# A third order for the repeated part of a linear-attention and ELU feed-forward kernel on one core

## The chip, the cores and the metric

One NeuronCore of one Trainium2 chip runs the program. The metric is device time in microseconds (us) of one execution; the span is the part of it between the first and the last instruction of the profile. Engines: TensorE (PE, its weight loads PEld), VectorE (DVE), ScalarE (ACT), GpSimd (POOL), SyncE (SP), which here only issues DMAs.

## The reference

Gated linear attention over 768 steps for 4 batches and 8 heads of width 48, then a feed-forward layer with an ELU on the 3072 tokens of width 384. All in float32.

```python
for t in range(S):                                   # q, k, v, alpha: (4, 8, 768, 48)
    state = alpha[:, :, t, :, None] * state + einsum('bhd,bhe->bhde', k[:, :, t], v[:, :, t])
    y[:, :, t] = einsum('bhd,bhde->bhe', q[:, :, t], state)
x = y.transpose(0, 2, 1, 3).reshape(3072, 384)
h = x @ w_in                                         # 384 x 2048
g = where(h > 0, h, exp(minimum(h, 0)) - 1)
out = g @ w_out                                      # 2048 x 384
```

## The kernel before

The sequence is cut into 24 windows of 128 steps (6 for each batch), handled in chunks of 64; the tokens into 12 blocks of 256, two windows each, and the hidden width into 8 pieces j of 256. Each step of the work is a small function, a token. A program text is a list of tokens with their index; START holds the tokens of the first part one by one, STEADY (L79) is a pattern that `steady()` (L761) repeats for g = 4 to 13 and that is cut off at both ends. Under `manual_schedule` each engine runs its instructions in the order of the list; between engines only data, buffers and semaphores order the work. So the list is ten queues of order at once, one for each engine, and the place of a token against tokens of other engines has no force by itself.

In STEADY the number behind a token counts from g: for A, RA, RB, RC, GH, GL and O it is 8 g + k, the piece j of a block (A.0 to A.4 are pieces 0 to 4 of block g, A.-3 to A.-1 pieces 5 to 7 of block g - 1; O.-5 is piece 3 of block g - 1); for CA, CB and LC it is 4 g + k; for Z it is the block; for the others the window 2 g + k.

The tokens, with their engine and line:

- Loads on SP, all on one queue in list order: L (L170, k, q and alpha of a window), LV (L183, v, two DMAs), LC (L593, a part of the weights, read again for a check), XD (L536, four small copies that fold y into the layout of x), Z's two stores (L709).
- Window work: SC (DVE, L195, a scan of alpha into P), LN and EX (ACT, L208, L213), KA and KB (POOL here, L221, L226), KC (DVE, L231), SQ (POOL here, L240), T.i.g (DVE, L288, four transposes of 32 x 32 blocks by its helper; four T a window), PC (ACT, L236, a sum for a check), ZV (POOL, L264).
- S (PE, L328) and U (PE, L374), 32 small matmuls each, write the two halves of the same two PSUM banks of a window. MK (DVE, L344, in two parts of two instructions) masks what S gave. UA, UB, UC (DVE, L416 to L428, two instructions each) form the state for the second chunk and for the next window from what U gave. UA of each sixth window is on ACT.
- Y (PE, L483, 32 matmuls), XH (ACT, L501) and XL (DVE, L521) make the two float32r halves of the feed-forward input xt of a block.
- Feed-forward: A (PE, L640, 18 matmuls of 128 x 256 into one bank h), RA and RB (ACT, L655, L661), RC (DVE, L666), GH (ACT, L672), GL (DVE in all blocks from 4 on, L682), O (PE, L692, 12 matmuls of 128 x 384 into the two banks of a block), Z (ACT and SP, L709).
- CA and CB (ACT, L599, L604) check the weights that LC loaded. V and VP come once, in block 11.

Buffers: one pool of 8 PSUM banks serves h, y, the pairs of U and S and the pairs of O; r, gh and gl have three buffers each (gh and gl are free again when their O has run), ck has one, P, R, kn, y3 and xt two, qka tiles three and v tiles four in rotation.

```python
h = psa.tile([128, 2, BLK], F32, name="h", tag="pa")                       # A
gh = d["gh"] = gpool.tile([128, 2, BLK], F32R, name="gh", tag="gh", bufs=3)  # GH
gl = d["gl"] = gpool.tile([128, 2, BLK], F32R, name="gl", tag="gl", bufs=3)  # GL
```

Of the kernel before, what the change touches and what calls it, by code (L numbers as in the profile page):

```python
# [14 lines left out]
B, H, S, D = 4, 8, 768, 48  # L15
# [61 lines left out]


STEADY = """  # L79
A.-3 Y.1 XH.1 Y.0 XH.0 A.-2 XL.1 RA.-3 O.-5 RA.-2 XL.0 LV.4 U.2 CA.-12 V.0 RB.-3 S.2 UA.2 MK.2.0 U.3 UB.2 S.3  # L80
MK.2.1 UC.2 XD.1 ZV.4 O.-4 XD.0 RC.-3 CB.-12 SC.4 RB.-2 A.-1 PC.3 GH.-3 RC.-2 A.0 LN.4 GL.-3 UA.3 EX.4 RA.-1
GH.-2 LC.-11 MK.3.0 L.6 MK.3.1 UB.3 CA.-11 A.1 RA.0 KA.4 L.5 RB.-1 GL.-2 RC.-1 A.2 RB.0 UC.3 CB.-11 RA.1 GH.-1
RC.0 O.-3 KB.4 RB.1 SC.5 KC.4 LC.-10 GL.-1 LN.5 GH.0 EX.5 RC.1 T.4.1 O.-2 A.3 VP.0 CA.-10 T.4.2 GL.0 GH.1 A.4
T.4.3 KA.5 O.0 RA.2 GL.1 RB.2 RA.3 CB.-10 LV.5 RC.2 PC.4 GH.2 KB.5 RB.3 GL.2 LC.-9 O.1 O.-1 KC.5 RA.4 O.2 SQ.4
T.5.2 CA.-9 RB.4 RC.3 CB.-9 RC.4 GH.3 T.5.1 GH.4 T.5.0 GL.3 T.4.0 T.5.3 LC.-8 SQ.5 Z.-1 GL.4
"""

@with_exitstack
# [882 lines left out]
```

## Time and profile before

| | |
|---|---|
| median of 3 runs | 479.66 us (479.53 to 479.87) |
| the profiled execution | 478.73 us, its span 476.8 us |
| PE busy / PEld busy | 469.3 us / 450.3 us |
| DVE / ACT / POOL busy | 380.0 / 299.2 / 124.0 us |
| granted TensorE clock | 1.00 in every slice |
| HBM | 53.53 MB read, 4.72 MB written, 122 GB/s |

A busy PE is not a PE at its peak: matmuls are pipelined and a matmul that starts late may show as a longer piece. Pieces of the same kind and count can be compared with each other. In the chain of waits a piece is one engine's run of instructions of one line; "x72" behind a line of A are four A, "x24" behind a line of O two O.

### The profile page before, as it was taken

To read this page: it belongs to the slowest core of one execution; us is meant where nothing else is said; L and a number is where in the kernel's file an instruction comes from. 1 tells how busy PE (TensorE), PEld (TensorE's weight loads), DVE (VectorE), ACT (ScalarE), POOL (GpSimd) and SP (SyncE) were. 2 spreads that over 40 slices of the span, in tenths; PEclk is the share of its full clock that TensorE was granted. 3 is DMA by queue.
4 is the path that set the end of the run, shared out by engine and by line. 5 is a ranking of instruction groups with operands and counts; after the bars stand their busy time and mean duration, and the time that the engine had idled before them with its cause. 6 is when DMAs were issued, how large, how long until landed. Compare 5 with 4: busy or idle time off the path is not lost.

```text
span 476.8 us, 13298 instructions
## 1 busy us (share of the span) xinstructions
PE 469.3 (98%) x5438; PEld 450.3 (94%) x5438; DVE 380.0 (80%) x770; ACT 299.2 (63%) x696; POOL 124.0 (26%) x111
## 2 busy tenths in 40 slices
PE   8999999999999999999999999999999999999995
PEld 4889999999999999999999999999999999999995
DVE  6989999789889979869989989878988998344321
ACT  4586668764764668756766765757765666554432
POOL 3012332534564602502602602602602500000000
PEclk9999999999999999999999999999999999999999
DMA  8999330712326056235235335334333321210011
GB/s 307 414 414 409 118 84 16 229 55 78 110 101 200 1 151 204 69 112 206 61 115 180 90 113 176 95 114 172 101 104 113 100 69 52 66 43 10 2 36 38
DMA packets 20483, 61.14 MB, mean 128 GB/s; under 512 B 2880, under 2 KB 7872, under 8 KB 20416
## 3 DMA queue, kind: packets, MB, share of 16 engines
q1 hardware_dynamic: 20128, 59.83, 37.3%
q8 instruction: 45, 0.74, 0.7%
q10 hardware_dynamic: 288, 0.39, 0.2%
q14 instruction: 22, 0.18, 0.1%
HBM read 53.53 MB, written 4.72 MB: 122 GB/s over the span
## 4 chain that ended last, share of the span: by engine, by line
PE 98%; ACT 0%; DVE 0%; POOL 0%; issue 0%; POOLq 0%; DVEq 0%
PE h L650 42%; PE o L703 39%; PE y L452 4%; PE q L368 2%; PE y L447 2%; PE q L323 2%; PE wp L126 2%; PE sc L339 1%; PE wd L623 1%; PE tp L274 1%; PE y L492 1%; PE u L386 1%; PE yl L447 0%; PE wd L511 0%; POOL gl L689 0%
## 5 line engine op out<-in xcount | busy, mean ns | idle before, releaser
L650 PE MATMUL h<-xt,w 128*128 128x256 f32 x1728 | 204.8, 277 | 0.5 <-DVE r L669 0.2
L650 PEld LDWEIGHTS h<-xt,w 128*128 128x128 f32 x1728 | 198.5, 192 | 4.2 <-issue 1.6
L703 PE MATMUL o<-w,gh 128*128 128x384 f32 x768 | 188.2, 327 | 0.0
L703 PEld LDWEIGHTS o<-w,gh 128*128 128x128 f32 x768 | 132.8, 189 | 0.5
L703 PE MATMUL o<-w,gl 128*128 128x384 f32 x384 | 125.6, 327 | 0.0
L658 ACT ACTIVATE r<-h 128x512 f32<-128x512 f32 x96 | 56.8, 594 | 41.7 <-PE h L650 34.5
L675 ACT CAST gh<-h 128x512 fp32r<-128x512 f32 x79 | 45.9, 583 | 58.4 <-DVE h L669 35.3
L284 DVE STREAM_TRANSPOSE kn<-qka 32x128 f32<-32x128 f32 x256 | 77.4, 302 | 4.0
L689 DVE TENSOR_TENSOR gl<-h,gh 128x512 fp32r<-128x512 f32 x79 | 54.1, 688 | 28.4 <-ACT gh L675 27.3
L703 PEld LDWEIGHTS o<-w,gl 128*128 128x128 f32 x384 | 72.6, 189 | 0.6
L223 POOL TENSOR_TENSOR qka<-qka,R 128x512 f32<-128x512 f32 x18 | 23.1, 1283 | 155.9 <-DVE gl L689 109.4
L669 DVE SCALAR_TENSOR_TENSOR h<-r,h 128x512 f32<-128x512 f32 x79 | 53.0, 688 | 12.1 <-ACT r L663 11.4
L663 ACT ACTIVATE r<-r 128x512 f32<-128x512 f32 x96 | 59.5, 634 | 0.9
L351 DVE TENSOR_TENSOR st<-q,mask 64x256 f32<-64x256 f32 x72 | 30.4, 422 | 9.0 <-ACT vs L403 7.2
L253 POOL TENSOR_TENSOR st<-qka,P 64x512 f32<-64x512 f32 x30 | 36.0, 1199 | 1.6
L228 POOL TENSOR_TENSOR R<-P,R 128x512 f32<-128x512 f32 x20 | 24.4, 1221 | 33.9 <-DVE qka L223 32.5
L689 POOL TENSOR_TENSOR gl<-r,gh 128x512 fp32r<-128x512 f32 x17 | 24.1, 1425 | 25.4 <-ACT gh L675 16.9
L201 DVE TENSOR_TENSOR_SCAN P<-qka,first 128x516 f32<-128x516 f32 x24 | 29.5, 1229 | 1.3 <-DMA qka<-in_qka_dram 0.8
L210 ACT ACTIVATE R<-P 128x512 f32<-128x512 f32 x24 | 15.1, 631 | 17.8 <-DVE P L201 17.8
L601 ACT ACTIVATE ck<-ck 128x384 f32<-128x384 f32 x32 | 22.2, 694 | 5.6 <-DMA ck<-in_wgt_dram 5.6
L606 ACT ACTIVATE ck<-ck,lim 128x384 f32<-128x384 f32 x32 | 24.6, 768 | 0.1
L233 DVE SCALAR_TENSOR_TENSOR qka<-R,qka 128x512 f32<-128x512 f32 x24 | 19.9, 827 | 1.5 <-POOL R L228 1.3
(105 smaller groups left out, 448.4 us busy)
## 6 DMA issues: line engine op xcount, KB each, us to landing
qka<-in_qka_dram SPq DMA_DIRECT2D x22, 770.0 KB, 5.6
raw<-in_wgt_dram SPq DMA_DIRECT2D x16, 768.0 KB, 13.4
ck<-in_wgt_dram SPq DMA_DIRECT2D x32, 384.0 KB, 3.3
vs<-in_vv_dram SPq DMA_DIRECT2D x36, 192.0 KB, 3.3
out_dram<-ot SPq DMA_DIRECT2D x22, 192.0 KB, 2.0
vs<-in_vv_dram SPq DMA_DIRECT2D x6, 384.0 KB, 9.9
xt<-y SPq DMA_DIRECT2D x40, 48.0 KB, 2.2
qka<-in_qka_dram SPq DMA_DIRECT2D x2, 512.0 KB, 4.8
```

The lines of the kernel that those rows point to most:

```text
L201: nc.vector.tensor_tensor_scan(out=P.rearrange("p n w -> p (n w)"), data0=t[:, 2 * NP * W:], data1=first.rearrange("p n w -> p (n w)"), in ...
L253: eng(SQV, i).tensor_tensor(out=st[r, a], in0=d["q"][r], in1=pw(i)[r], op=ALU.mult)
L284: nc.vector.transpose(out=kn[32 * t:32 * t + 32, :, 32 * g:32 * g + 32], in_=d["kt"][32 * g:32 * g + 32, :, 32 * t:32 * t + 32])
L351: nc.vector.tensor_tensor(out=d["st"][r, a, :, c * C:(c + 1) * C], in0=d["s4"][a][o], in1=mask[o].unsqueeze(1).broadcast_to([64, NP, C]), ...
L606: nc.scalar.activation(out=t, in_=t, func=AF.Relu, scale=-1.0, bias=lim, accum_out=chk_w[:, 1, f:f + 1])
L650: nc.tensor.matmul(h[:, f, :], lhsT=t[:, wi, ws], rhs=x[:, :, c, xi].rearrange("p a x -> p x a"), start=(f == 0 and k == 0), stop=(k == 8) ...
L658: nc.scalar.activation(out=r, in_=d["h"], func=AF.Relu, scale=-1.0)
L663: nc.scalar.activation(out=d["r"], in_=d["r"], func=AF.Exp, scale=-1.0)
L669: nc.vector.scalar_tensor_tensor(out=d["g"], in0=d["r"], scalar=-1.0, in1=d["h"], op0=ALU.add, op1=ALU.max)
L675: nc.scalar.copy(out=gh, in_=d["g"])
L689: q.tensor_tensor(out=gl, in0=d["g"], in1=d["gh"].bitcast(F32), op=ALU.subtract)
L703: nc.tensor.matmul(o[:, 0:DM], lhsT=gt[:, f, ms], rhs=t[:, wi, f * DM:f * DM + DM].rearrange("p (a x) -> p x a", a=2), start=(j == 0 and f ...
```

## The change

Only the text STEADY changes. It holds the same 122 tokens in both versions, each once, in another order; START, the token functions, tiles, buffers and the repeat are the same.

```diff
 STEADY = """
-A.-3 Y.1 XH.1 Y.0 XH.0 A.-2 XL.1 RA.-3 O.-5 RA.-2 XL.0 LV.4 U.2 CA.-12 V.0 RB.-3 S.2 UA.2 MK.2.0 U.3 UB.2 S.3
-MK.2.1 UC.2 XD.1 ZV.4 O.-4 XD.0 RC.-3 CB.-12 SC.4 RB.-2 A.-1 PC.3 GH.-3 RC.-2 A.0 LN.4 GL.-3 UA.3 EX.4 RA.-1
-GH.-2 LC.-11 MK.3.0 L.6 MK.3.1 UB.3 CA.-11 A.1 RA.0 KA.4 L.5 RB.-1 GL.-2 RC.-1 A.2 RB.0 UC.3 CB.-11 RA.1 GH.-1
-RC.0 O.-3 KB.4 RB.1 SC.5 KC.4 LC.-10 GL.-1 LN.5 GH.0 EX.5 RC.1 T.4.1 O.-2 A.3 VP.0 CA.-10 T.4.2 GL.0 GH.1 A.4
-T.4.3 KA.5 O.0 RA.2 GL.1 RB.2 RA.3 CB.-10 LV.5 RC.2 PC.4 GH.2 KB.5 RB.3 GL.2 LC.-9 O.1 O.-1 KC.5 RA.4 O.2 SQ.4
-T.5.2 CA.-9 RB.4 RC.3 CB.-9 RC.4 GH.3 T.5.1 GH.4 T.5.0 GL.3 T.4.0 T.5.3 LC.-8 SQ.5 Z.-1 GL.4
+Y.1 XH.1 Y.0 XL.1 A.-1 RA.-1 A.-3 RA.-3 RB.-3 A.-2 RC.-3 XH.0 XL.0 GH.-3 O.-5 GL.-3 ZV.4 V.0 RB.-1 RC.-1 CA.-12
+CB.-12 U.2 XD.1 S.2 MK.2.0 UA.2 UB.2 RA.-2 UC.2 MK.2.1 SC.4 RB.-2 RC.-2 LN.4 EX.4 U.3 XD.0 GH.-2 LV.5 S.3 LC.-11
+CA.-11 L.5 CB.-11 O.-4 O.-3 A.0 RA.0 MK.3.0 UA.3 MK.3.1 UB.3 UC.3 GL.-2 GH.-1 RB.0 A.1 PC.3 GL.-1 LC.-10 RC.0 A.2
+KA.4 KB.4 L.6 RA.2 RB.2 A.3 RA.3 SC.5 SQ.5 KC.4 T.4.2 T.4.0 O.-2 VP.0 RA.1 RB.1 LC.-9 SQ.4 GH.0 CA.-10 PC.4 GL.0
+RC.1 CB.-10 GH.1 RC.2 GL.1 LV.4 GH.2 A.4 RB.3 RC.3 LN.5 EX.5 GL.2 T.4.3 KA.5 KB.5 GH.3 GL.3 RA.4 RB.4 O.-1 RC.4
+GH.4 KC.5 CA.-9 CB.-9 T.5.2 O.0 T.5.3 T.5.0 O.1 O.2 Z.-1 LC.-8 GL.4 T.4.1 T.5.1
 """
```

Taken apart by engine:

| engine | before | after |
|---|---|---|
| PE | A.-3 Y.1 Y.0 A.-2 O.-5 U.2 S.2 U.3 S.3 O.-4 A.-1 A.0 A.1 A.2 O.-3 O.-2 A.3 VP A.4 O.0 O.1 O.-1 O.2 | Y.1 Y.0 A.-1 A.-3 A.-2 O.-5 U.2 S.2 U.3 S.3 O.-4 O.-3 A.0 A.1 A.2 A.3 O.-2 VP A.4 O.-1 O.0 O.1 O.2 |
| SP | LV.4 XD.1 XD.0 LC.-11 L.6 L.5 LC.-10 LV.5 LC.-9 LC.-8 Z.-1 | XD.1 XD.0 LV.5 LC.-11 L.5 LC.-10 L.6 LC.-9 LV.4 Z.-1 LC.-8 |
| DVE | XL.1 XL.0 V UA.2 MK.2.0 UB.2 MK.2.1 UC.2 RC.-3 SC.4 RC.-2 GL.-3 UA.3 MK.3.0 MK.3.1 UB.3 GL.-2 RC.-1 UC.3 RC.0 SC.5 KC.4 GL.-1 RC.1 T.4.1 T.4.2 GL.0 T.4.3 GL.1 RC.2 GL.2 KC.5 T.5.2 RC.3 RC.4 T.5.1 T.5.0 GL.3 T.4.0 T.5.3 GL.4 | XL.1 RC.-3 XL.0 GL.-3 V RC.-1 MK.2.0 UA.2 UB.2 UC.2 MK.2.1 SC.4 RC.-2 MK.3.0 UA.3 MK.3.1 UB.3 UC.3 GL.-2 GL.-1 RC.0 SC.5 KC.4 T.4.2 T.4.0 GL.0 RC.1 RC.2 GL.1 RC.3 GL.2 T.4.3 GL.3 RC.4 KC.5 T.5.2 T.5.3 T.5.0 GL.4 T.4.1 T.5.1 |
| POOL | ZV.4 KA.4 KB.4 KA.5 KB.5 SQ.4 SQ.5 | ZV.4 KA.4 KB.4 SQ.5 SQ.4 KA.5 KB.5 |
| ACT | XH.1 XH.0 RA.-3 RA.-2 CA.-12 RB.-3 CB.-12 RB.-2 PC.3 GH.-3 LN.4 EX.4 RA.-1 GH.-2 CA.-11 RA.0 RB.-1 RB.0 CB.-11 RA.1 GH.-1 RB.1 LN.5 GH.0 EX.5 CA.-10 GH.1 RA.2 RB.2 RA.3 CB.-10 PC.4 GH.2 RB.3 RA.4 CA.-9 RB.4 CB.-9 GH.3 GH.4 Z.-1 | XH.1 RA.-1 RA.-3 RB.-3 XH.0 GH.-3 RB.-1 CA.-12 CB.-12 RA.-2 RB.-2 LN.4 EX.4 GH.-2 CA.-11 CB.-11 RA.0 GH.-1 RB.0 PC.3 RA.2 RB.2 RA.3 RA.1 RB.1 GH.0 CA.-10 PC.4 CB.-10 GH.1 GH.2 RB.3 LN.5 EX.5 GH.3 RA.4 RB.4 GH.4 CA.-9 CB.-9 Z.-1 |

## Rows read from the trace of the kernel before

**Rows 1.** The page, busy time (share of the span) xinstructions: TensorE and its loads.
```profile
PE 469.3 (98%) x5438; PEld 450.3 (94%) x5438; DVE 380.0 (80%) x770; ACT 299.2 (63%) x696; POOL 124.0 (26%) x111
```

**Rows 2.** Chain of waits in order of time: start us, us, what.
```profile
215.67 8.39 PE h L650 x72
224.07 3.90 PE o L703 x24
...
231.99 7.90 PE o L703 x48
...
241.89 2.02 PE y L452 x64
243.91 2.21 PE h L650 x18
...
248.06 0.51 PE q L368 x32
...
252.10 8.45 PE h L650 x72
...
397.98 8.28 PE h L650 x72
...
432.11 8.04 PE h L650 x72
```

**Rows 3.** Timeline of VectorE: start us, us, engine, line, operation, out<-in [idle before].
```profile
231.34 0.69 DVE L689 TENSOR_TENSOR gl<-h,gh 128x512 fp32r<-128x512 f32 x1
...
253.81 1.23 DVE L201 TENSOR_TENSOR_SCAN P<-qka,first 128x516 f32<-128x516 f32 x1
255.54 0.68 DVE L689 TENSOR_TENSOR gl<-h,gh 128x512 fp32r<-128x512 f32 x1
256.86 1.75 DVE L351 TENSOR_TENSOR st<-q,mask 64x256 f32<-64x256 f32 x4
263.39 0.67 DVE L233 SCALAR_TENSOR_TENSOR qka<-R,qka 128x512 f32<-128x512 f32 x1
272.45 0.88 DVE L233 SCALAR_TENSOR_TENSOR qka<-R,qka 128x512 f32<-128x512 f32 x1
273.37 1.25 DVE L284 STREAM_TRANSPOSE kn<-qka 32x128 f32<-32x128 f32 x4
282.49 0.55 DVE L533 TENSOR_TENSOR xt<-y,xt 128x384 fp32r<-128x384 f32 x1
285.59 0.72 DVE L405 TENSOR_TENSOR vs<-vs,q 48x192 f32<-48x192 f32 x2 [1.90 <-PE q L323]
```

**Rows 4.** Busy time by stretch: PE, PEld, DVE, ACT, POOL (xinstructions), PEclk, DMA share, GB/s.
```profile
252.10:288.60 36.50, 36.42 (x416) 35.42 (x417) 32.66 (x77) 24.37 (x60) 10.16 (x10) 1.00 0.41 132
```

**Rows 5.** The page's groups: line, engine, operation xcount | busy, mean ns | idle before, releaser.
```profile
L675 ACT CAST gh<-h 128x512 fp32r<-128x512 f32 x79 | 45.9, 583 | 58.4 <-DVE h L669 35.3
L669 DVE SCALAR_TENSOR_TENSOR h<-r,h 128x512 f32<-128x512 f32 x79 | 53.0, 688 | 12.1 <-ACT r L663 11.4
L663 ACT ACTIVATE r<-r 128x512 f32<-128x512 f32 x96 | 59.5, 634 | 0.9
```

**Rows 6.** Waits: engine, line <- releaser: us in total, times, longest us.
```profile
ACT gh L675 <- PE o L703: 28.8, 19, 3.5
```

**Rows 7.** The page's DMA issues: out<-in, queue, xcount, KB each, us to landing.
```profile
qka<-in_qka_dram SPq DMA_DIRECT2D x22, 770.0 KB, 5.6
ck<-in_wgt_dram SPq DMA_DIRECT2D x32, 384.0 KB, 3.3
```

**Rows 8.** Timeline of GpSimd, SQ of the block from 252.10.
```profile
267.81 4.96 POOL L253 TENSOR_TENSOR st<-qka,P 64x512 f32<-64x512 f32 x4
```

**Rows 9.** Timeline of ScalarE at the border of START and STEADY.
```profile
172.58 0.26 ACT L506 ACTIVATE y<-y 128x128 fp32r<-128x128 f32 x1
```

## The prediction

> **What bounds the kernel now.** I read three views in this order. First the page's table of busy time: TensorE has matmuls for 98% of the span [rows 1], no other engine is near it. Second the chain of waits in order of time: from 124 us on nearly every piece of it is TensorE itself, so the time is the sum of TensorE's pieces, and a change of order, which adds and removes no instruction, can only win what lies in these pieces beyond their least price. The reader is to see that the pieces of one kind differ [rows 2]. Four A in a row (72 matmuls) take 8.39, 8.45 and 8.28 us in blocks that also run U and S, and 8.04 in the block that has none; so an A is 2.01 us at its least. Four O in a row take 7.90, where two take 3.90, so 1.95 each. The first A behind Y costs 2.21, 0.20 more, for the change from narrow to full matmuls. Third, VectorE's timeline beside that: it says what the excess is [rows 3]. In the four A that begin at 252.10, A.1 is due at 252.10 + 2 x 2.01 = 256.1, and takes the PSUM bank that GL.-3 gives back at 255.54 + 0.68 = 256.2; A.2 is due at 258.2 and takes one that MK.3 gives back at 256.86 + 1.75 = 258.6. The two delays make 0.4, and 8.45 - 8.04 = 0.41. In the four O from 231.99, the GL that O.0 reads ends at 231.34 + 0.69 = 232.03, just too late: 0.1. **So the loss is a VectorE that hands on late by tenths**, and it has little room: 32.66 us busy of a block's 36.50 [rows 4].
>
> **The least time of a block.** 8 A x 2.01 = 16.08, 0.20 behind Y, 7 O x 1.95 = 13.65, two Y 2.02, and the stretch U, S, U, S, O.-4 with its waits, 248.06 to 252.10, 4.04 (its clean form 4.00): 35.95. A block takes 252.10 - 215.67 = 36.43 [rows 2]. So 0.48 is to be had in each of six whole blocks, and 8.28 - 8.04 = 0.24 in the last of the seven that run U and S: 6 x 0.48 + 0.24 = 3.1 us. The order after keeps Y, Y, A together and U, S, U, S, O together, so both changes of shape stay paid once a block.
>
> **What the new order does, TensorE first.** With t = 0 at Y.1 and no waits: Y.0 1.0, A.-1 2.0, A.-3 4.2, A.-2 6.2, O.-5 8.2, U.2 10.2, S.2 ends 11.2, S.3 ends 12.1, O.-4 to 14.2, O.-3 to 16.2, A.0 16.2, A.1 18.2, A.2 20.2, A.3 22.2, O.-2 24.2, A.4 26.2, O.-1 28.2, O.0 30.1, O.1 32.1, O.2 34.0, end 36.0. Now I ask of each whether its input or bank is there.
>
> **VectorE from S.2's end.** MK.2, UA.2, UB.2, UC.2, SC.4, RC.-2, MK.3, UA.3, UB.3, UC.3: MK 2 x 1.75, six of UA, UB, UC at 0.72, SC 1.23, RC 0.69 [rows 3, 5]: 9.7, so UC.3 ends at 20.9 to 21.1. A.2 takes the bank that MK.3.1 releases (19.1, due 20.2) and A.3 the one of UC.3 (due 22.2): about 1.1 us to spare, where before there was none. (Banks go in order of release: six are free at a block's start, so each allocation takes the sixth last release.) GL.-2, GL.-1 at 0.69, RC.0, SC.5 1.23, KC.4 0.7, T.4.2 and T.4.0 1.26 each: GL.0 ends at 28.0, O.0 is due at 30.1. RC.1, RC.2, GL.1: 30.0, O.1 due 32.1.
>
> **ScalarE's new waits.** gh has three buffers, so GH.2, GH.3, GH.4 must wait for O.-1 (ends 30.1), O.0 (32.1), O.1 (34.0): a wait that the list adds on purpose, with RB.3, LN.5, EX.5, RA.4, RB.4 queued behind the first. The trace has this wait already, 28.8 us in 19 times, without harm to TensorE [rows 6]. GH.2 0.58, RB.3 0.63 [rows 5]: RB.3 ends at 31.3, so RC.3 waits 1.4 us on VectorE; RC.3 0.69, GL.2 0.69: 32.7, O.2 due 34.0. To spare 1.3. The other long waits of ScalarE cost nothing: RA.-1 waits for A.-1 (4.2) and RA.-3 for A.-3 (6.2), with XH.0 behind them until 7.4; LN.4 waits for SC.4 (16.4) with GH.-2 and CA.-11 behind it, and GH.-2 ends at 18.2, GL.-2 comes at 21.1, O.-2 at 24.2.
>
> **VectorE over the block's end.** RC.3 at 31.3, then four RC, four GL, KC.5, six T, two XL: 4 x 0.69 + 4 x 0.69 + 0.8 + 6 x 1.26 + 2 x 0.8 = 15.5, with overlaps of neighbours 15.1: RC.-1 ends at 46.4, and S.2 of the next block ends at 36.0 + 11.2 = 47.2. To spare 0.8. On the way RC.-3 waits for RB.-3, which A.-3 dates (7.4); VectorE gets there at 7.6, so nothing is lost. From GH.2 to A.3's bank the loop so has 0.8 + 1.1 = 1.9 us before TensorE sees a delay.
>
> **The loads.** SP now issues both pairs of XD first, then LV.5, LC.-11, L.5, LC.-10, L.6, LC.-9, LV.4, Z, LC.-8, and each LC waits for CB of the one before, with the loads queued behind it. L.5 goes at about 12 and lands 5.6 later, 18 [rows 7]; SC.5 comes at 23. L.6 goes at about 20, SC.4 of the next block comes at 51. LV.4 goes behind LC.-9, which waits for CB.-10 (28.4): landed by 33, wanted by U.2 at 46. LC.-10 goes at 19.5 and lands at 23, CA.-10 comes at 26.3 [rows 7]. XD.0 goes at 9.1 behind XL.0, A.0 reads its tile at 16.2. Z.-1 moves behind CB.-9 and ends at 2.0 of the next block; its banks go to A.-3 at 4.2. All are covered by over 1 us; uncovered, an L would cost up to its 5.6 in each block.
>
> **A rule against it.** KC.4 now stands beside SQ.5 on GpSimd. A KC beside SQ took 0.88, one alone 0.67 [rows 3, 8]: 0.2 us, which RC.3's wait of 1.4 swallows. The Trainium skill (SBUF — State Buffer, Who interferes with whom) says that a VectorE instruction with two SBUF inputs and a GpSimd instruction that reads SBUF shut each other out for a whole instruction. By it KC.4 could lose a whole SQ piece, 4.96 / 4 = 1.24 us [rows 8], still under 1.4; the trace agrees, as the KC that took 0.88 began before SQ ended.
>
> **The edges.** At the border to START, ScalarE is free for XH.1 at 172.58 [rows 9]; Y would begin near 167, as the A that stood ahead of it is moved behind. From 172.58: XH, RA, RA, RB, XH, GH, RB, some 5.2 us, then RC.-1: MK.2 at 178.5, S.2 over at 178.2; 0.3 late, under the 1.1 to spare. Where START's last O interleave with the first tokens of STEADY, narrow Y now may stand between O: 0 to three changes of 0.20, I take 0.2. Block 11 has no U and S and no excess (8.04); the tail keeps its sum, O of the last block coming last either way, GH of the last but two by their O: nothing.
>
> **Sum.** The profiled execution took 478.73 (span 476.8), the median of the three runs is 479.66. -3.1 + 0.2 = -2.9: 475.8 by the profiled run, 476.8 by the median, which is what I give.
>
> **Rivals.** (1) No change: VectorE's waits come back elsewhere. Its busy 32.66 leaves 3.3 of 36.0, and I spend 0.8 + 1.4 + short ones of some 1.0 on waits. If the loop is 2.0 to 2.7 us longer than my sum, TensorE loses 0.1 to 0.8, on average the old 0.45: 479.7. For it: all instructions were taken at their plain durations. Against it: RC.3's wait is there to take lateness up. (2) Slower: ScalarE's queue becomes the bound. O.-1, GH.2, RB.3, RC.3 and the 15.1 us to MK.2 and 9.7 to UC.3, then A.3, are one loop over a block. It decides from 1.9 + 0.45 = 2.3 us above my sum; at 3.0 above it TensorE loses 1.1 in seven blocks, 7.7, less the 3.1: 484.3. For it: GH.2 waits for its O in every block, where 19 such waits stood in all. Against it: 3.0 is 11% of the loop's 27 us, and the durations scatter by a few per cent. (3) That late loads are not covered: a qka load of 5.6 us issued at 12 would have to land after 23; TensorE would lose in every block. I give it 0.03, within the slower ones.
>
> **Chances.** My forecast, faster by 2 to 3.5 us: 0.62. A part of it, 1 to 2 us: 0.08. Rival 1: 0.16. Rivals 2 and 3: 0.14. About 0.2% (0.96 us) is what a measurement can tell from no change: faster 0.69, same 0.17, slower 0.14. The range: below, the whole 3.1 with no cost at the border and 0.6 of hidden waits in U and S, 475.9; above, rival 1 and the mild part of rival 2: 481.0.
>
> **What would show it.** The four A at 8.04 to 8.1 and O at 1.95 in every block; blocks of 36.0; GH waiting for O three times a block, VectorE idle before RC.3. Wrong, if VectorE's idle time ahead of MK.2 is gone and A.2, A.3 or O.2 are longer than 2.01 and 1.95.

## The result, and the profile after

The changed kernel takes **475.57 us** (median of 4 runs, 475.21 to 475.72), the kernel before, run beside it, 479.6 us (479.48 to 479.87): ratio 0.9912, 95% interval 0.9897 to 0.9928. Forecast was 476.8 us, range 475.9 to 481.0. The direction was right, the gain is 4.0 us where 2.9 had been worked out, and the time lies 0.3 us below the lower end of the range. The profiled execution took 475.45 us, its span is 473.7 us.

The page of the changed kernel, busy time (share of the span) xinstructions, answering [rows 1]:

```profile
PE 466.6 (98%) x5438; PEld 449.3 (95%) x5438; DVE 381.1 (80%) x770; ACT 303.9 (64%) x696; POOL 126.3 (27%) x111
```

TensorE has the same 5438 matmuls and is busy 2.7 us less; VectorE has the same 770 instructions and is busy 1.1 us more. So no work is gone: the pieces on TensorE are shorter. The chain of waits of the changed kernel (start us, us, what), answering [rows 2], first the border of START and STEADY and then one block:

```profile
155.68 7.80 PE o L703 x48
163.48 0.26 PE y L452 x2
163.74 0.52 PE o L703 x2
164.26 0.27 PE y L452 x4
164.53 3.77 PE o L703 x22
168.30 1.89 PE y L452 x58
170.19 6.22 PE h L650 x54
...
256.18 8.04 PE h L650 x72
264.22 1.95 PE o L703 x12
266.17 2.01 PE h L650 x18
268.18 7.80 PE o L703 x48
275.98 2.02 PE y L452 x64
278.00 6.22 PE h L650 x54
284.22 1.95 PE o L703 x12
286.18 0.51 PE q L368 x32
...
288.00 4.10 PE o L703 x24
292.09 8.04 PE h L650 x72
```

Four A take 8.04 us in every block, where [rows 2] had 8.28 to 8.45 in the blocks with U and S; four O take 7.80, where they had 7.90; three A behind Y take 6.22, which is 3 x 2.01 and the 0.20 for the change from narrow to full matmuls. From 256.18 to 292.09 a block takes 35.91 us, and all whole blocks are alike (35.91 to 35.98): six of them with the short last one go from 184.28 to 433.73, 249.45 us, where the kernel before had 252.87 (179.24 to 432.11). Only the border, 163.48 to 170.19, is cut into small pieces of Y and O.

VectorE in the same block (start us, us, engine, line, operation [idle before]), answering [rows 3]:

```profile
264.18 0.67 DVE L233 SCALAR_TENSOR_TENSOR qka<-R,qka 128x512 f32<-128x512 f32 x1
...
271.16 0.70 DVE L669 SCALAR_TENSOR_TENSOR h<-r,h 128x512 f32<-128x512 f32 x1 [1.04 <-ACT r L663]
...
284.48 0.55 DVE L533 TENSOR_TENSOR xt<-y,xt 128x384 fp32r<-128x384 f32 x1
284.95 0.68 DVE L689 TENSOR_TENSOR gl<-h,gh 128x512 fp32r<-128x512 f32 x1
...
287.21 0.86 DVE L351 TENSOR_TENSOR st<-q,mask 64x256 f32<-64x256 f32 x2 [0.98 <-PE q L323]
```

The reader is to see the two places where VectorE now stands idle in every whole block: 1.04 us ahead of RC.3 (1.04 to 1.50 in the six) and 0.98 us ahead of MK.2. The second place alone is not what is new: the kernel before had 1.90 us of idle time there, ahead of UA.2 [rows 3]. So VectorE carried no lateness from one block into the next even then; its lateness arose anew between S.2 and the four A. What is new is when TensorE asks: O.-4 alone stood between S.3 and the four A, now O.-4 and O.-3 do, so that the four A come 1.95 us later.

To say where the 4.0 us went, I cut four profiled executions at two points that all kernels share: the start of START's last four O, and the end of ScalarE's last copy of out (L712).

| stretch | before | before, once more | after | after, once more |
|---|---|---|---|---|
| up to START's last four O | 155.32 | 156.01 | 155.68 | 155.59 |
| from there to the end of the last copy | 317.17 | 317.19 | 314.48 | 314.40 |
| from there to the end of the execution | 6.24 | 6.35 | 5.29 | 5.29 |
| time | 478.73 | 479.55 | 475.45 | 475.28 |

The middle row is the order's own doing: -2.7 us, which is -3.42 in the blocks and +0.72 at the border. The last row gives another -1.0. It holds two things: in the span the stretch behind the last copy falls from 4.31 and 4.30 to 3.54 and 3.61 us, and the time outside the span (time less span) from 1.93 and 2.05 to 1.75 and 1.68. The first row is START, which the change doesn't touch; it differs by 0.7 between two executions of the same kernel.

### The profile page after: what moved, and what is told of

Same layout as the page of the kernel before. It is cut to its first block, busy times and chain, and to the rows that moved or that the text cites. A ratio compares the mean times of both kernels' runs of the same rounds, so it can differ in the third digit from the quotient of the medians.

```text
span 473.7 us, 13243 instructions
## 1 busy us (share of the span) xinstructions
PE 466.6 (98%) x5438; PEld 449.3 (95%) x5438; DVE 381.1 (80%) x770; ACT 303.9 (64%) x696; POOL 126.3 (27%) x111
## 4 chain that ended last, share of the span: by engine, by line
PE 96%; ACT 1%; DVE 1%; DMA 1%; POOL 0%; issue 0%; POOLq 0%; DVEq 0%
PE h L650 41%; PE o L703 40%; PE y L452 4%; PE q L368 2%; PE y L447 2%; PE q L323 2%; PE wd L623 1%; PE sc L339 1%; PE tp L274 1%; PE y L492 1%; DMA qka<-in_qka_dram 1%; PE u L386 1%; DVE P L201 1%; PE yl L447 0%; ACT R L215 0%; PE wd L511 0%
## 5 line engine op out<-in xcount | busy, mean ns | idle before, releaser
L650 PE MATMUL h<-xt,w 128*128 128x256 f32 x1728 | 201.1, 276 | 0.2 <-DVE r L669 0.2
L663 ACT ACTIVATE r<-r 128x512 f32<-128x512 f32 x96 | 60.6, 635 | 1.9
L253 POOL TENSOR_TENSOR st<-qka,P 64x512 f32<-64x512 f32 x30 | 38.0, 1268 | 23.0 <-DVE P L201 13.5
L606 ACT ACTIVATE ck<-ck,lim 128x384 f32<-128x384 f32 x32 | 23.1, 721 | 0.7
```

Source lines behind the costliest of these rows:

```text
L253: eng(SQV, i).tensor_tensor(out=st[r, a], in0=d["q"][r], in1=pw(i)[r], op=ALU.mult)
L650: nc.tensor.matmul(h[:, f, :], lhsT=t[:, wi, ws], rhs=x[:, :, c, xi].rearrange("p a x -> p x a"), start=(f == 0 and k == 0), stop=(k == 8) ...
L663: nc.scalar.activation(out=d["r"], in_=d["r"], func=AF.Exp, scale=-1.0)
```

## The experiments

**1. The kernel before once more.** No edit; 479.55 us.

> The kernel before, once more, for a second trace of it. The prediction took 3.1 us from its profiled execution (478.73) and set them against the median of the timed runs (479.6). Theory A (the ordinary runs of the kernel before lose more in their blocks than the profiled one did, because VectorE is late by an amount that varies): the trace shows 479.2 to 479.9 in all, and its whole blocks take 36.55 us and more instead of 36.43 to 36.50. Theory B (the 0.9 us between profile and median lie in START or behind the last matmul, which both kernels share): the blocks take 36.43 to 36.50 again, and the stretch before 155 us or the one behind the last matmul is longer.

Its four A, in the chain of waits:

```profile
252.81 8.45 PE h L650 x72
289.31 8.47 PE h L650 x72
```

Blocks are as in the first execution (from 179.93 to 398.69, 218.76 us; before 218.74). The 0.82 us between the two executions are all in START (0.69) and behind the last copy (0.11). So the profiled execution of 478.73 us had an early START, and the excess is the same in both executions.

**2. In the kernel before, SC.4 later.** The prediction read two stalls of 0.2 us in the four A: A.1 for GL.-3, and A.2 for MK.3. Here SC and what follows it go behind MK.3, to give VectorE 1.23 us ahead of both.

```diff
-...O.-4 XD.0 RC.-3 CB.-12 SC.4 RB.-2 A.-1 PC.3 GH.-3 RC.-2 A.0 LN.4 GL.-3 UA.3 EX.4 RA.-1 GH.-2 LC.-11 MK.3.0 L.6
-MK.3.1 UB.3 CA.-11 A.1 RA.0 KA.4 L.5 RB.-1 GL.-2 RC.-1 A.2 RB.0 UC.3...
+...O.-4 XD.0 RC.-3 CB.-12 RB.-2 A.-1 PC.3 GH.-3 RC.-2 A.0 GL.-3 UA.3 RA.-1 GH.-2 LC.-11 MK.3.0 L.6
+MK.3.1 SC.4 UB.3 CA.-11 A.1 RA.0 L.5 RB.-1 GL.-2 RC.-1 A.2 RB.0 LN.4 EX.4 KA.4 UC.3...
```

> The kernel before with one thing moved on VectorE: SC.4 (1.23 us) goes from ahead of RC.-2, GL.-3 and MK.3 to behind MK.3, with LN.4, EX.4 and KA.4 behind it; TensorE's order is untouched. Theory (the excess of a block is TensorE waiting in A.1 for the bank of GL.-3 and in A.2 for the bank of MK.3): the four A in a row go from 8.45 to 8.04 in each block that runs U and S, and the time falls by 2.5 to 3.0 us, to about 477. Rival (the excess belongs to this order of TensorE's instructions, or to the loads of L that land at that time): no change.

Measured: 482.3 us (481.81 to 482.52), 3.0 us slower than the kernel before beside it, ratio 1.0056 (1.0043 to 1.0069). The expectation was wrong. Busy time in two stretches of four A (stretch, length, PE, PEld, DVE, ACT, POOL, PEclk, DMA share, GB/s):

```profile
253.94:262.22 8.28, 8.28 (x74) 8.28 (x75) 7.98 (x17) 5.61 (x12) 0.17 (x1) 1.00 0.52 211
290.82:299.10 8.28, 8.28 (x74) 8.28 (x75) 8.08 (x17) 5.61 (x12) 0.17 (x1) 1.00 0.49 181
```

The timeline of VectorE: SC.5 and GL.0 of the block from 253.94, then SC.5 and KC.4 of the block from 290.82:

```profile
263.99 1.70 DVE L201 TENSOR_TENSOR_SCAN P<-qka,first 128x516 f32<-128x516 f32 x1
...
270.05 0.69 DVE L689 TENSOR_TENSOR gl<-h,gh 128x512 fp32r<-128x512 f32 x1
...
299.07 1.22 DVE L201 TENSOR_TENSOR_SCAN P<-qka,first 128x516 f32<-128x516 f32 x1
302.66 0.69 DVE L233 SCALAR_TENSOR_TENSOR qka<-R,qka 128x512 f32<-128x512 f32 x1 [2.37 <-POOL R L228]
```

GpSimd's timeline, KB.4 of the block from 253.94:

```profile
263.41 1.18 POOL L228 TENSOR_TENSOR R<-P,R 128x512 f32<-128x512 f32 x1
```

TensorE's timeline, O.0 of that block:

```profile
270.79 0.43 PE L703 MATMUL o<-w,gl 128*128 128x384 f32 x1 [0.33 <-DVE gl L689]
```

And the waits of TensorE's loads from 165 us on (us in total, times, longest):

```profile
PEld o L703 <- DVE gl L689: 4.3, 6, 0.9
```

Four A fall from 8.45 to 8.28 us with TensorE's order untouched, so a stall of 0.17 there did come from VectorE being late, but only one of the two named: with MK.3 and GL.-3 both earlier, 0.24 stays. The traces say where. A's matmuls and loads in the kernel before, in stretches of 0.40 us (stretch, length, PE, PEld, PEclk, DMA share, GB/s); a stretch without a wait holds 6 matmuls or 7:

```profile
251.90:252.30 0.40, 0.20 (x2) 0.23 (x3) 1.00 0.94 300
...
255.90:256.30 0.40, 0.40 (x6) 0.30 (x4) 1.00 0.78 323
256.30:256.70 0.40, 0.40 (x4) 0.40 (x4) 1.00 0.30 92
...
258.30:258.70 0.40, 0.40 (x6) 0.40 (x5) 1.00 0.00 0
```

VectorE's MK.2.1, which ends just ahead of the four A, in the kernel before and in this run:

```profile
251.53 0.88 DVE L351 TENSOR_TENSOR st<-q,mask 64x256 f32<-64x256 f32 x2
```

```profile
253.36 0.88 DVE L351 TENSOR_TENSOR st<-q,mask 64x256 f32<-64x256 f32 x2
```

There is a hole at A.1 (due at 256.1, its bank free when GL.-3 ends at 256.22), and none at A.2 (258.3), in any block. The other stall is at A.-1: its load waits on VectorE's semaphore and starts at 252.07, 0.11 us after the first half of MK.2.1 ended at 251.96; in this run, where MK.2 is in its old place, it starts at 253.90, 0.12 us after 253.79. Taken matmul by matmul, the block from 252.10 to 288.60 loses 0.17 us at A.1, 0.10 at O.0 and 0.31 at the next A.-1, 0.58 of the 0.59 by which it is longer than 35.91. In this run A.1 has no hole; in the changed kernel neither place has one.

And the gain is more than eaten. KA.4 and KB.4 follow SC.4 on GpSimd and come late with it. In four of six blocks SC.5 then runs beside KB.4 (263.41 to 264.59) and takes 1.70 us, where a scan alone takes 1.22; in the two others, whose second window is the last of its batch and has no UB and UC, VectorE is further on and KC.4 waits 2.37 us for KB.4. Either way what follows on VectorE is late: GL.0 ends at 270.05 + 0.69 = 270.74, O.0 waits for it and starts at 270.79. The six blocks take 36.88 to 37.13 us, 221.74 together (179.91 to 401.65), 3.0 more than the 218.74 of the kernel before. The Trainium skill (SBUF — State Buffer, Who interferes with whom) says that a VectorE instruction with two SBUF inputs contends with a GpSimd instruction that reads SBUF, for ports that are locked exclusively; this row agrees to 0.1 us, a scan held until KB.4 ends would end at 264.59 + 1.22 = 265.81, it ended at 265.69. What follows: the old order had no room on VectorE there. In these four blocks O.0 stands about 0.6 us longer than in the kernel before (0.48 of delay on VectorE, and TensorE itself 0.17 earlier), and a block is 0.4 longer. A single move doesn't get the gain, since it hands the lateness on.

**3. START and STEADY in one list.** The prediction took 0.2 us at the border. If the interleaving of Y and O there is the cost, one list removes it.

```diff
-    with tc.manual_schedule():
```
(the second of two such lines, at L754, so that the tokens of STEADY stand in the same list as those of START)

> The changed kernel with START and STEADY under one manual schedule instead of two, so that no Y of the first block stands between the O of START. The trace of the changed kernel has 6.71 us from the first such Y to the last, for matmuls that take 3.90 + 2.02 elsewhere. Theory (each change from narrow Y to full O costs about 0.2 us): Y comes in one piece, 0.6 to 0.8 us less, 474.9. Rival (without Y in between TensorE waits there for the GL that O reads): no change, 475.6.

> The changed kernel with START and STEADY in one scheduled list, for a comparison in the same group as the changed kernel. In its first execution Y lay in one piece of 2.02 us at the border and the saving there was 0.6 to 0.7 us. Theory: 0.4 to 0.8 us below the changed kernel, 474.7 to 475.1. Rival: the piece at the border is saved, but the time is the same within 0.2, as the length of START scatters by more than that.

Measured: 474.93 us (474.16 to 476.99), ratio 0.9911 (0.9894 to 0.9928), and in the second group 475.71 us (474.2 to 477.29), ratio 0.9931 (0.9912 to 0.9951), where the changed kernel beside it had 475.25 us (475.0 to 477.49). The chain of waits of the second execution:

```profile
155.29 11.70 PE o L703 x72
167.00 2.02 PE y L452 x64
```

Y is in one piece and six O take 11.70, as little as they can (6 x 1.95). From START's last four O to the last copy this kernel takes 313.62 us (313.64 in the first execution), the changed kernel 314.40: 0.78 us are saved, which is 6.71 - (3.90 + 2.02) = 0.79 at the border. In the medians the two kernels can't be told apart, as three of its six times lie 2 us above the other three (see below). The border's term is thus 0.8, and this is the fastest version seen, by its trace and by its lowest time, not by its median.

**4. The loads of the old order.** Only SP's queue is put back: LV.4 behind Y.0, L.6 and L.5 behind LC.-11, LV.5 behind LC.-10. (LC.-8 stays behind Z.-1, as in the new order.)

```diff
-Y.1 XH.1 Y.0 XL.1 A.-1 ... GH.-2 LV.5 S.3 LC.-11 CA.-11 L.5 CB.-11 ... GL.-1 LC.-10 RC.0 A.2 KA.4 KB.4 L.6 ... GL.1 LV.4 GH.2
+Y.1 XH.1 Y.0 LV.4 XL.1 A.-1 ... GH.-2 S.3 LC.-11 L.6 L.5 CA.-11 CB.-11 ... GL.-1 LC.-10 LV.5 RC.0 A.2 KA.4 KB.4 ... GL.1 GH.2
```

> The changed kernel with SP's queue as it was before: LV.4 right behind Y.0, L.6 and L.5 together behind LC.-11, LV.5 behind LC.-10. Theory (all loads are covered by over 1 us in either place): no change, 475.6, and four A in a row stay at 8.04. Rival (the spread of the loads is a part of the gain, as L.6 and L.5 together delay LC, CA and with them ScalarE): slower by 0.4 us a block, 478.

Measured: 475.49 us (475.23 to 478.1), ratio 0.9938 (0.9917 to 0.9959). Its chain of waits:

```profile
255.90 8.04 PE h L650 x72
267.89 7.80 PE o L703 x48
...
291.80 8.04 PE h L650 x72
```

Blocks of 35.90 to 35.92 and 314.40 us to the last copy, as in the changed kernel. The spread of the loads is no part of the gain; in both orders they are covered.

**5 and 6. The end alone.** The pattern of the last repeat (g = 12) is taken from the other kernel.

```diff
-        for x in STEADY.split():
+        for x in (STEADY if g < NBLK else TAIL).split():
```
(TAIL is the STEADY of the other version)

> The changed kernel, with the order of before in the last repeat alone (g = 12: A of pieces 5, 6, O, O, A of piece 7, O, O, O instead of three A and then five O). TensorE's work there is the same 15.8 us without a wait in both. Theory (the end behind the last matmul is 0.7 us shorter in the span and 0.3 us outside it after the change, because with three A first VectorE and ScalarE are through 4.7 us ahead of the last matmul instead of 2.2, and what the engines fetch and branch to at their end no longer falls on the last store): slower by 0.7 to 1.0 us than the changed kernel, 476.4, and the last store lands after 2.5 us instead of 1.9. Rival (the end differs by chance from run to run): no change, 475.5.

> The kernel before, with the changed order in the last repeat alone. Theory (as for the tail of before in the changed kernel): faster by 0.7 to 1.0 us, 478.5, the last store lands after 1.9 us. Rival: no change, 479.4.

Measured: the changed kernel with the old end 476.24 us (475.81 to 476.68), ratio 0.9930 (0.9917 to 0.9943), 0.7 us above the first median of the changed kernel; the kernel before with the new end 478.83 us (478.44 to 480.79), 0.67 below the kernel before beside it, but ratio 0.9992 with an interval of 0.9981 to 1.0003. By these times alone neither exchange can be told from noise (the changed kernel itself had 0.9912 in one group and 0.9929 in the other); what follows rests on the traces. The last two stores in the kernel before (DMA issues: queue, xcount, KB each, median us from issue to landing):

```profile
out_dram<-ot ACTq DMA_DIRECT2D x2, 192.0 KB, 2.5
```

The same in the changed kernel:

```profile
out_dram<-ot ACTq DMA_DIRECT2D x2, 192.0 KB, 1.9
```

In the changed kernel with the old end:

```profile
out_dram<-ot ACTq DMA_DIRECT2D x2, 192.0 KB, 2.7
```

And in the kernel before with the new end:

```profile
out_dram<-ot ACTq DMA_DIRECT2D x2, 192.0 KB, 1.9
```

TensorE's sum is the same with either end: 314.41 us to the last copy with the old one, 314.40 with the new. What differs lies behind the last copy: 6.24 us with the old end in the changed kernel, 5.29 with the new. In the kernel before, the new end brings the landing to 1.9 as well, but the rest behind the copy only falls from 6.24 and 6.35 to 6.11. So the landing goes with the end's order: 2.5 to 2.7 us in all four traces with the old end, 1.9 in nine of ten with the new (the tenth is in the last section). A part of the last row does not go with it: the time outside the span is 1.8 to 2.1 us in every timed execution of the kernel before, also with the new end, and 1.7 to 1.8 in every one of the changed kernel, also with the old; what sets it no run shows. In the span the exchange costs the changed kernel 1.0 us (3.54 and 3.61 to 4.56) and saves the kernel before 0.2 (4.30 to 4.10), and that difference stays open. A store that shares its time with instructions being fetched is a candidate: behind the last copy one instruction queue carries 2 packets in each trace with the old end and 1 in each with the new. But the packets and the order change together, so it isn't shown.

**7 to 10. How much room VectorE has.** The prediction gave the loop from GH.2 to A.3 a room of 1.9 us. Four transposes of a window that are done again add 1.26 us to VectorE in each of six blocks, and change nothing else. They are put behind RC.3's wait (T.5.1 twice, then three times), and ahead of it (T.4.0 twice, then three times).

```diff
-... GL.4 T.4.1 T.5.1
+... GL.4 T.4.1 T.5.1 T.5.1
```
(and with a third T.5.1)
```diff
-... KC.4 T.4.2 T.4.0 O.-2 ...
+... KC.4 T.4.2 T.4.0 T.4.0 O.-2 ...
```
(and with a third T.4.0)

> The changed kernel with T.5.1 written twice: VectorE gets 1.26 us more work in each of the six blocks that prepare windows, and nothing else changes. Theory (VectorE has two waits in a block that take up lateness, 0.98 us ahead of MK.2 and 1.04 us ahead of RC.3 in the trace of the changed kernel, 2.0 in all): no change, within 0.5 us; the wait ahead of MK.2 is gone and four A in a row stay at 8.04. Rival (any lateness of VectorE reaches TensorE, as in the kernel before): slower by up to 6 x 1.26 = 7.6 us.

> The changed kernel with T.5.1 written three times: 2.53 us more VectorE work in each of the six blocks. Theory: the two waits take up 2.0, the rest of 0.5 comes through in each block, some of it swallowed once by the 1.1 us to spare at A.3: slower by 1.5 to 3 us, 477 to 478.5, blocks of 36.4. Rival (VectorE has more room than that, the waits are not what keeps TensorE free): no change.

> T.4.0 is written twice (four transposes are done again), 1.26 us more VectorE work in each of six whole blocks, but ahead of the wait of RC.3 (1.04 us) and not behind it as in the run where T.5.1 was doubled. Theory (the idle time ahead of RC.3 takes up what comes before it; the margin at U is 1.15 us): RC.3 comes 0.2 us late, U is not touched, GL.0 ends near 269.4 where O.0 is due at 270.1: no change, 475.2 to 475.8. Rival (a block has one sum of slack, wherever the work stands): as with T.5.1 doubled, +0.9, 476.3.

> T.4.0 is written three times, 2.53 us more in each block, ahead of the wait of RC.3. Theory: GL.0 ends near 270.65, 0.5 us after O.0 is due at 270.13, and this 0.5 is lost in each block; what comes behind is then late by 2.53 - 1.04 = 1.5, less the 0.5 by which TensorE is late as well, 1.0, which the 1.15 at U take up. So +0.5 a block, +3 us: 478.2 to 479. Rival (one sum of slack): as with T.5.1 written three times, +8.0, 483.5.

| kernel | time, us (range) | ratio (interval) | six blocks against the changed kernel |
|---|---|---|---|
| T.5.1 twice | 476.41 (475.65 to 476.55) | 0.9930 (0.9917 to 0.9943) | +0.3 |
| T.5.1 three times | 483.5 (482.91 to 485.57) | 1.0094 (1.0077 to 1.0112) | +7.8 |
| T.4.0 twice | 477.32 (475.45 to 478.24) | 0.9949 (0.9931 to 0.9968) | 0.0 |
| T.4.0 three times | 478.94 (478.16 to 480.82) | 1.0004 (0.9992 to 1.0017) | +3.0 |

The last column comes from the chain of waits, from the first four A of STEADY to those six blocks on (changed kernel, second execution, 215.48 us; T.5.1 three times 184.45 to 407.69, 223.24; T.4.0 twice 215.51, three times 218.49). The expectation for T.5.1 three times, 477 to 478.5 us, was wrong: it counted the waits of VectorE as one sum. U.3 in TensorE's timeline of that run, in the block from 259.07:

```profile
290.59 0.56 PE L368 MATMUL q<-vs,kn 64*48 64x48 f32 x16 [0.26 <-DVE xt L533]
```

The waits of TensorE's loads and of TensorE over these blocks with T.4.0 three times (us in total, times, longest):

```profile
PEld o L703 <- DVE gl L689: 2.6, 4, 1.0
PE o L703 <- DVE gl L689: 1.4, 2, 0.7
```

And VectorE's timeline with T.5.1 three times, at the same place of a block:

```profile
274.04 0.70 DVE L669 SCALAR_TENSOR_TENSOR h<-r,h 128x512 f32<-128x512 f32 x1 [0.79 <-ACT r L663]
...
283.22 5.19 DVE L284 STREAM_TRANSPOSE kn<-qka 32x128 f32<-32x128 f32 x16
...
289.89 0.55 DVE L533 TENSOR_TENSOR xt<-y,xt 128x384 fp32r<-128x384 f32 x1
290.44 0.69 DVE L689 TENSOR_TENSOR gl<-h,gh 128x512 fp32r<-128x512 f32 x1
```

Behind RC.3, 2.53 us more cost 1.3 a block, and TensorE waits at U and S. They take the banks that XL.1, XL.0 and GL.-3 give back, and the traces say which takes which. The expectations paired XL.0 with the start of U.2 (a room of 1.15 us). But with T.5.1 twice XL.0 ended 0.12 us after U.2 had begun, and U.3 began on time. With T.5.1 three times U.2 began on time at 288.99; it was U.3 that waited for XL.0 (ended 290.44, U.3 from 290.59), and behind it the last bank waited for GL.-3 (ended 291.13). In the changed kernel U.3 starts at 286.98, 1.95 us after XL.0 has ended, and the bank of GL.-3 (ended 285.63) is taken at 287.26 by S.3, a room of 1.6, or, where U.3 has both its halves, some 0.2 sooner, a room of 1.4. So GL.-3 decides: 2.53 less 1.6 or 1.4 is 0.9 or 1.1, and the blocks took a little more than that, 1.08 us in the two with half a U.3 and 1.40 in the four others. VectorE still stands idle 0.79 us ahead of RC.3, but that wait can't help: it lies ahead of the added work, and it is tied to O.-1, which moves with TensorE. Ahead of RC.3, the same 2.53 us cost 0.5 a block in the mean, and TensorE waits at O.0 for GL.0 and under 0.1 us at U: GL.0 ended at 268.12 (267.43 + 0.69) in the changed kernel, O.0 is due at 268.18 + 1.95 = 270.13; 2.53 more make it 0.5 late. By block it is not 0.5: O.0 stood 0.3, 1.0, 0.4 and 1.0 us in four blocks, and not at all in the two whose second window is the last of its batch, as VectorE has less to do there. RC.3's wait and the room at U take up the rest. One lot of 1.26 us is under both rooms, and the blocks don't change beyond 0.05 each. The rival with one sum of slack for the block gave 483.5 for T.4.0 three times; measured 478.94. The rooms are places.

The times of the runs with a lot of 1.26 us (476.41 and 477.32) are 1 to 2 us above the changed kernel's all the same. That is not in the blocks: with T.5.1 twice START was 0.5 longer in the profiled execution, and the stretch behind the last copy 0.3, all of it outside the span (1.9 to 2.1 us there in every execution of these two kernels); with T.4.0 twice the profiled execution has 7.9 us behind the last copy instead of 5.29.

**The changed kernel once more** stood beside the last three as their measure.

> The changed kernel once more, beside which the three others of this group stand. Expected from its earlier executions: 475.2 to 475.7 us. It also says how far two groups of runs of one kernel lie apart, which bounds what can be said of differences of a few tenths.

Measured: 475.25 us (475.0 to 477.49), ratio 0.9929 (0.9911 to 0.9947). The two groups of runs agree to 0.3 us.

## Why the prediction was right, and where it was wrong

- **What bounds the kernel: right.** In the blocks the pieces of one kind differed by VectorE's lateness: in the block taken apart under experiment 2 it accounts for 0.58 of 0.59 us, and in the new order all pieces are at their least. The chain of waits is TensorE from 156 us to the last copy. The reason given, a VectorE with little room over a block (32.66 us busy of 36.50), is not what the rows show: it stood idle 1.90 us just ahead of the stretch in which it then was late.
- **The least time of a block: right, mis-sized by a little.** 35.95 was forecast, 35.91 to 35.98 measured (35.93 in the mean). The excess was 0.48 a block by one block of 36.43; blocks of 36.38 to 36.50 stand beside it (36.46 in the mean), and so the whole is 3.42 where 3.1 had been worked out. One block was taken for six.
- **The walk through a block: right.** Forecast idle time was 1.4 us ahead of RC.3 and 0.8 ahead of MK.2; measured 1.04 to 1.50 and 0.98. GH waits for an O 11 times (12.7 us in all from 165 us on), not three times a block, and delays nothing on TensorE. KC.4 beside SQ took 0.67 us, not 0.88: it began at 264.18, SQ at 264.40.
- **The room: wrong, without harm to the forecast.** "From GH.2 to A.3's bank the loop so has 0.8 + 1.1 = 1.9 us": the walk asked for the banks of A.2 and A.3, but not for those of U, which XL and GL.-3 release. There the room is 1.4 to 1.6 (experiments 7 and 8). The point from which rival 2 would decide lay that much nearer.
- **The split of the old stalls: half wrong.** The sum of 0.41 in the four A was right. A.1's share, put down to GL.-3, is there: 0.17. A.2's, put down to MK.3, is not: A.2 starts on time in every block, and the other 0.24 is at the start of A.-1, which waits for MK.2 (experiment 2). It was luck that the sum came out; it took no harm, since the new order relieves A.-1 as well.
- **The border: too small.** "0 to three changes of 0.20, I take 0.2": it is 0.72 to 0.79, by four changes between Y and O, shown by experiment 3. The row at the border was there to be drawn up: TensorE's list at that point alternates Y and O.
- **The tail: the step that failed.** "The tail keeps its sum: nothing" is right for TensorE up to the last copy (314.41 against 314.40) and wrong for what follows: from the last copy to the end it is 1.0 us less. The prediction asked only when the last O and GH come, and not what comes behind them. About 0.7 of it is in the span; experiment 5 ties that to the order of the last repeat by one trace, in which the old end brings it back, while in the kernel before the new end gives only 0.2 of it. The other 0.25 lies outside the span and does not follow the end's order. The cause of either stays open.
- **Sum and range.** Forecast -3.1 + 0.2 + 0 = -2.9. Measured in profiled executions: -3.42 + 0.72 - 1.0 = -3.7 without START. The remaining 0.3 of the 4.0 is the difference between medians and profiled executions; START scatters by more than that, so it can't be placed. The range's lower end took in hidden waits in U and S, but nothing at the tail, so it ended 0.3 too high.
- **The rivals fell.** No change and the slower one would both need waits of TensorE in STEADY; there are none over 0.2 us. Rival 3, late loads, fell with them; experiment 4 adds that neither order of SP's queue shows in the blocks.

## What to carry to other kernels

Where one engine is busy 98% of the span, compare its pieces of one kind with each other; what lies above the least of them is what an order can win there, and the sum of the excess over every block, not over one, is the forecast. Look for each stall between the single matmuls before you name its cause: here the pieces gave the sum, and one of the two places was wrong. The room of the engine behind it isn't one number for the block: write down for each hand-over (inputs and banks alike) when it is ready and when it is due, and mind that a wait takes up only what comes before it on its engine. And cost both ends of a repeated part as well: here the border and the last store made up 1.7 us of changes, of opposite sign, beside 3.4 in the blocks.

## What the runs showed of the hardware

START is the same in all these kernels, and its last four O began at 155.3 to 156.2 us in the profiled executions. A part of the difference may be there from the first microseconds on: the last of the 25 warm-up matmuls (L126) started at 8.6 to 10.1 us. It isn't all of it: in the two executions of the kernel before it started at 9.12 and 9.29 us, and START was 0.69 apart. About 0.9 us of scatter between executions is thus made by no order. The last store of out scatters too. It landed after 1.9 us in all but one of the profiled executions with the new end; in the execution with T.4.0 twice its two stores took 3.1 us in the median, the last of them 4.2:

```profile
out_dram<-ot ACTq DMA_DIRECT2D x2, 192.0 KB, 3.1
```

and the time was 478.16, where blocks as good as the changed kernel's should have given 475.5. Times 2 us above the rest stand in several of the groups (477.49 of the changed kernel, 476.66 to 477.29 of the single list, 480.26 to 480.82 of T.4.0 three times); that these are late stores as well is possible, but none of them was profiled. The mean granted clock of most of them is also lower (0.995 to 0.998); it was 0.997 in the execution with T.4.0 twice, whose blocks were no longer than the changed kernel's. So differences under 1 us between these kernels are read from the blocks in the trace, and not from medians.
